# Program order for the first slots, and a weight conversion in two steps, in a delta-rule and MoE kernel

## The chip, the cores and the metric

The kernel runs on one core of one Trainium2 chip. The metric is the device time of one execution in microseconds, the median of three runs. Before the change it is 869.11 us (the three runs: 869.25, 866.1, 869.11). The profile is of another execution, which took 863.97 us and spans 862.2 us from its first to its last instruction.

## What is computed

Two blocks follow each other. The first is a delta-rule recurrence over 768 positions for 4 batches of 8 heads of width 48; the second is a two-layer block with a quick GELU over the 3072 resulting tokens, 384 to 2048 to 384.

```python
for t in range(S):                       # 768 positions, per batch and head
    kt, vt, bt = k_n[:, :, t], v[:, :, t], beta[:, :, t, None]
    y[:, :, t] = einsum('bhd,bhde->bhe', q[:, :, t], state)
    v_old = einsum('bhde,bhd->bhe', state, kt)
    state = state + bt[:, :, :, None] * einsum('bhd,bhe->bhde', kt, vt - v_old)
x = y.transpose(0, 2, 1, 3).reshape(3072, 384)
h = x @ w_in
out = (h / (1 + exp(-1.702 * h))) @ w_out
```

Here k_n is k divided by its norm. The activations q, k, v and beta are float32. The weights w_in and w_out arrive as 64-bit floats[...], so the kernel turns their two 32-bit words into float32 itself.

## The kernel before, in words

The positions are cut into 6 chunks of 128. A **unit** is one chunk of one batch with its 8 heads; there are 24, in the order chunk by chunk, so units 0 to 3 are the first chunk of the four batches, units 4 to 7 the second. Within a chunk the recurrence is solved in 4 blocks of 32 positions.

What a unit needs:

- `normalize` divides its keys by their norms. The first seven units are done on DVE by `normalize_first`; later ones mostly on POOL.
- `prepare` transposes keys and queries on PE (psT), copies them with ACT to kqT, multiplies them (psG) and copies the products to G with ACT or DVE. A part of G goes through DRAM to NT, and POOL masks the rest with affine_select.
- `invert` turns NT into the inverses of the 32 x 32 diagonal blocks, on DVE; they go through DRAM and come back as XB.
- The class `Step` solves the unit: `above` (PE, psR), `rest` (DVE subtracts psR from V), `solve` (PE, psU from XB and V) and `solved` (ACT copies psU to U), block after block; then `state` (PE psS, DVE adds it to S_bd) and `outputs` (PE psY, ACT and DVE copy it to xT, and six small DMAs move some of its rows).
- `hidden` (PE ph from xT and w_in, ACT's GELU to gT) and `written` (PE po from gT and w_out) are the second block. They wait in a list, `queue`, and `take` draws from it by cost.

The loop at the end of the program calls `slot(n)` for n from -1 to 24. A slot has six groups. In it three units are in work side by side: A = unit n-1 (blocks 2 and 3, state, outputs), B_ = unit n (block 1) and D_ = unit n+1 (block 0). Each group also prepares a piece of unit n+4, inverts a piece, converts some weight parts and draws from `queue`; while `queue` is still empty, it issues six bf16 products on the identity (`warm`) that keep PE busy.

**Weights.** w_in is 12 parts of 128 x 512, w_out 16 parts of 128 x 384. `fetch` brings a part's 64-bit words into a stage, most of which lies in the memory of w_out itself, whose final values come later; `taken` records which words of it are in use, and `ahead` fetches a part only if its stage is free. `convert` calls `from_double`, and `made` frees a stage, for most parts one part later. `from_double` is, for a part that is not among the first three: DVE masks the exponent (L167), ACT shifts it and clamps it at zero with a ReLU (L172), DVE builds the mantissa from the high word (L173) and the low word (L174), puts the sign to the exponent (L175) and multiplies the two (L176). The first three parts (`alone`) do the ReLU's work with two DVE operations. `weights(n)` converts n parts and fetches ahead. How many parts are converted where is set by W0 (before the slots), W1 (just before the loop) and WB (slots -1 to 3).

**What sets the order on an engine.** The program's order is not the order of the queues. A scheduler takes the instructions by priority and by when it expects them to be ready, so it moves an instruction ahead of earlier ones that it thinks have to wait. An operation wrapped in `pinned` is kept behind the pinned ones before it on its engine. Before the change only the work of the first chunk's inversion, of `normalize_first`, of the first three conversions and some DMAs are pinned:

```python
def pinned(op):
    return lambda *a, **kw: tc.keep_in_program_order(op(*a, **kw))
```

Pinned instructions carry the wrapper's line, L104, in the profile. As built before, PE's queue holds, after the 48 warm products of `invert`, another 36 of slots -1 and 0, then all of `prepare` for units 4, 5 and 6 with more warm products, and only then the first `solve`. ACT's queue has the same units' copies ahead of the first U.

Of the kernel before, what the change touches and what calls it, by code (L numbers as in the profile page):

```python
# [18 lines left out]
def kernel(  # L19
# [19 lines left out]
    nc = tc.nc  # L39
# [18 lines left out]
    W0, W1, WB = 3, 2, (1, 3, 4, 7, 8)  # L58
# [46 lines left out]

    for i in range(B):
        for t, src, dma in ((KN, k, nc.sync.dma_start), (QP, q, nc.scalar.dma_start)):
            if i < len(t):
                nc.vector.memset(t[i][:, :, D:DP], 0.0)
                load(i, ((t, src),), dma)  # L110
# [21 lines left out]
    def warm(n, after=None):  # L132

        ps = ps_moe.tile([128, 256], F32, tag="moe", name="ps_warm")
        if after is not None:
            after(ps[:, 0:1], 0.0)
        for _ in range(n):
            nc.tensor.matmul(ps, lhsT=ones[:, 0:128], rhs=ones, start=True, stop=True)  # L138
# [11 lines left out]
    def from_double(dst, raw, n, alone):  # L150

        lo, hi = raw[:, :, 0], raw[:, :, 1]
        tmp = wk.tile([128, 2, n], I32, tag="P", name="tmp")
        t0, p = tmp[:, 0], tmp[:, 1]  # L160
        ts, stt = nc.vector.tensor_scalar, nc.vector.scalar_tensor_tensor
        if alone:
            ts, stt = pinned(ts), pinned(stt)
        AND, OR = ALU.bitwise_and, ALU.bitwise_or
        E1 = 1 << 20

        ts(p, hi, 0x7FF * E1, None, op0=AND)  # L167
        if alone:
            ts(p, p, -896.0 * E1, 0.0, op0=ALU.add, op1=ALU.max)
            ts(p, p, 255.0 * E1, 8.0, op0=ALU.min, op1=ALU.mult)  # L170
        else:
            nc.scalar.activation(p, p, ACT.Relu, scale=8.0, bias=low)  # L172
        ts(t0, hi, E1 - 1, E1, op0=AND, op1=OR)  # L173
        stt(out=dst, in0=lo.bitcast(U32), scalar=2.0**-32, in1=t0, op0=ALU.mult, op1=ALU.add)  # L174
        stt(out=p, in0=hi, scalar=-(1 << 31), in1=p, op0=AND, op1=OR)  # L175
        stt(out=dst, in0=dst, scalar=2.0**-20, in1=p.bitcast(F32), op0=ALU.mult, op1=ALU.mult)  # L176
# [16 lines left out]
    stages, taken, made = {}, {}, []  # L193
# [61 lines left out]

    def convert(part):
        if part in stages:
            dst = target(part)
            from_double(dst, stages.pop(part), dst.shape[-1], part < NA)

            made.append(part)
            while made and (len(made) > 1 or part < NA or part >= n_parts - 8):
                taken.pop(made.pop(0), None)
# [5 lines left out]
    def normalize(n):  # L269
# [6 lines left out]
        nc.vector.tensor_reduce(ssq, ksq, axis=AX.X, op=ALU.add)  # L276
# [3 lines left out]
        nc.vector.tensor_scalar(rn, rn, 1e-6, None, op0=ALU.add)  # L280
        nc.vector.reciprocal(rn, rn)
# [3 lines left out]
    def normalize_first(b0, nb=HB):  # L285

        tt, ts = pinned(nc.vector.tensor_tensor), pinned(nc.vector.tensor_scalar)
        red, recip = pinned(nc.vector.tensor_reduce), pinned(nc.vector.reciprocal)
        stt = pinned(nc.vector.scalar_tensor_tensor)
# [21 lines left out]
    def prepare(n):  # L311
# [4 lines left out]
        for i, src in enumerate((kn, qp)):  # L316
# [5 lines left out]
            for j in range(NP):  # L322
                nc.tensor.transpose(psT[:, j, :], flat[:, j * 128 : (j + 1) * 128], ident)  # L323
            nc.scalar.activation(kqT[:, :, i, :], psT, ACT.Copy)  # L324
# [4 lines left out]
        for g in range(0, NP, 2):  # L329
# [4 lines left out]
            for i in range(2):  # L334
                for hh in range(2):
                    pr = slice(hh * 64, hh * 64 + D)
                    nc.tensor.matmul(  # L337
                        ps[hh][:, i], lhsT=kqT[pr, g + i, 0, :], rhs=kqT[pr, g + i, :, :],
                        start=True, stop=True,
                    )  # L340
            nc.scalar.activation(G[:, 2 * g : 2 * g + 4 : 2], ps[0], ACT.Copy)  # L341
            if n < HB or B <= n < 2 * B + HB:
                nc.scalar.activation(G[:, 2 * g + 1 : 2 * g + 4 : 2], ps[1], ACT.Copy)
            else:
                nc.vector.tensor_copy(G[:, 2 * g + 1 : 2 * g + 4 : 2], ps[1])  # L345
# [22 lines left out]
    def invert(c, b0=0, nb=B):  # L368
# [5 lines left out]
        tt, red = nc.vector.tensor_tensor, nc.vector.tensor_reduce  # L374
# [35 lines left out]
        nc.scalar.activation(X1, halves(Y)[1].rearrange("p l i -> p i l"), ACT.Copy)  # L410
# [21 lines left out]
        if c == 0:  # L432
            warm(NY, pinned(nc.vector.memset))
        YS = wk.tile([128, BS, BS], F32, tag="P", name="YS")[part]
        nc.vector.tensor_tensor(YS, Y, bc, op=ALU.mult)
# [21 lines left out]
    class Step:  # L457
# [10 lines left out]
        def with_state(self, ps, i):  # L468
            for j in range(NP):
                nc.tensor.matmul(  # L470
# [8 lines left out]
        def above(self, blk, h):  # L479
            r, a = slice(blk * BS, (blk + 1) * BS), slice(0, blk * BS)  # L480
            nc.tensor.matmul(  # L481
# [4 lines left out]
        def rest(self, blk):  # L486
            r = slice(blk * BS, (blk + 1) * BS)
            if self.c > 0 or blk > 0:
                nc.vector.tensor_tensor(self.V[r], self.V[r], self.psR[r], op=ALU.subtract)  # L489

        def solve(self, blk, h, psU):
            r = slice(blk * BS, (blk + 1) * BS)
            nc.tensor.matmul(  # L493
# [4 lines left out]
        def solved(self, blk, psU):  # L498
            r = slice(blk * BS, (blk + 1) * BS)
            nc.scalar.copy(self.U[r], psU[r])  # L500

        def turned(self, lhsT, rhs, start):

            for h in range(H):
                j, p = h // 2, h % 2 * 64
                nc.tensor.matmul(  # L506
# [13 lines left out]
        def state(self):  # L520
# [3 lines left out]
            for j in range(NP):  # L524
                nc.tensor.matmul(  # L525
# [4 lines left out]
            for hh in range(2):  # L530
                pr = slice(hh * 64, hh * 64 + 64)
                St = S_bd[pr, self.b, :, hh, :]
                nc.vector.tensor_tensor(St, psS[pr, :, hh, :], St, op=ALU.add)

        def outputs(self):
# [6 lines left out]
            other = nc.scalar.copy if self.c == 0 else nc.vector.tensor_copy  # L542
            for hh, copy in ((0, nc.scalar.copy), (1, other)):
# [14 lines left out]
    def hidden(xT, gT, t, cost):  # L558

        n = t.stop - t.start  # L560
        for f0 in range(0, FC, 2):
# [3 lines left out]
            for u in range(2):  # L565
                f = f0 + u
                for j in range(KC):
                    nc.tensor.matmul(  # L568
# [4 lines left out]
            nc.scalar.activation(  # L573
# [3 lines left out]
    def written(c, b0, gT):  # L577

        for i in range(HB):
            b = b0 + i  # L580
            po = ps_moe.tile([128, DM], F32, tag="moe", name="po")
            for f in range(FC):
                nc.tensor.matmul(  # L583
# [6 lines left out]
            nc.vector.tensor_copy(o, po)  # L590
# [166 lines left out]
    for n in range(-1, len(units) + 1):  # L757

# [32 lines left out]
```

## Time and profile before

| engine | busy us | share of the span |
|---|---|---|
| PE, products | 806.3 | 94% |
| PE, weight loads | 597.2 | 69% |
| DVE | 490.7 | 57% |
| ACT | 208.7 | 24% |
| POOL | 105.5 | 12% |

Shares of the whole span hide that the kernel has stages. In the table of busy times by stretch PE is at 0.00 us busy from 40 to 60 us, where DVE inverts the first chunk's blocks, and at 20.00 of 20.00 us in each stretch from 200 to 320 us. By line, the chain of work that ended last is PE ph 29.5%, PE po 28.0%, and for the rest mostly the recurrence's products; DMA of w_out's words has 1.6%. Of the waits, the longest single one on DVE that a conversion causes is 8.1 us, for ACT's ReLU (L172); ACT in turn waited 43.4 us in 14 waits for DVE's mask (L167), which costs nothing where ACT had nothing else to do.

In the profile a row of a timeline gives the start, the duration, the engine and line, what is written from what, how many instructions are merged, and in brackets how long the engine had stood idle before and what released it. PE stands for TensorE's products, PEld for its weight loads.

### The profile page before, as it was taken

How to read it: one execution, taken by the hardware profiler on the slowest of the kernel's cores; microseconds unless marked ns; L12 is line 12 of the kernel's file. 1: busy time of each engine (PE TensorE's matmuls, PEld its weight loads, DVE VectorE, ACT ScalarE, POOL GpSimd, SP SyncE). 2: the span in 40 equal slices, each digit the busy share in tenths (PEclk: the TensorE clock that was granted, in tenths of full speed). 3: DMA queues.
4: the chain of work that ended last, by engine and by line, in shares of the span. 5: the costliest groups of instructions: out<-in, count | busy, mean ns of one | idle time of the engine just before them, and what ended most of it. 6: DMA issues, size and time to landing. Idle time of an engine off the chain costs nothing.

```text
span 862.2 us, 15547 instructions
## 1 busy us (share of the span) xinstructions
PE 806.3 (94%) x6564; PEld 597.2 (69%) x6564; DVE 490.7 (57%) x1024; ACT 208.7 (24%) x407; POOL 105.5 (12%) x117
## 2 busy tenths in 40 slices
PE   8209799989999999999999999999999999999998
PEld 7107678757767867867767767767768768677684
DVE  5897579979982692682782772772862851110100
ACT  3202345433212312312312212212212112112020
POOL 2103131330012102102102101101100000000000
PEclk9759769999999999999999999999999999999999
DMA  9996462541423123132132132042032020000000
GB/s 144 185 165 148 109 162 68 141 112 33 83 60 68 40 58 73 35 73 60 34 76 65 26 85 62 19 85 53 10 78 50 2 57 2 10 14 1 19 5 18
DMA packets 160964, 55.75 MB, mean 65 GB/s; under 512 B 128672, under 2 KB 157568, under 8 KB 160896
## 3 DMA queue, kind: packets, MB, share of 16 engines
q1 hardware_dynamic: 154048, 46.02, 26.1%
q0 software_dynamic: 1856, 7.87, 3.0%
q10 hardware_dynamic: 4992, 0.89, 1.0%
q8 instruction: 51, 0.84, 0.4%
q14 instruction: 17, 0.14, 0.1%
HBM read 33.13 MB, written 20.45 MB: 62 GB/s over the span
## 4 chain that ended last, share of the span: by engine, by line
PE 83%; DVE 8%; DMA 5%; issue 1%; ACT 1%; ACTq 0%; POOL 0%; SPq 0%; DVEq 0%; POOLq 0%
PE ph L568 30%; PE po L583 28%; PE psR L481 5%; PE psY L506 5%; PE psG L337 5%; PE psU L493 4%; PE psR L470 2%; PE psS L525 2%; PE psT L323 2%; DMA w_out<-in_moe_w_out_dram 2%; DMA w_out<-in_moe_w_in_dram 1%; DVE P L104 1%; DMA bI<-in_beta_dram 1%; DVE YB L104 1%; DMA Nd<-G 1%
## 5 line engine op out<-in xcount | busy, mean ns | idle before, releaser
L583 PE MATMUL po<-w_out,gT 128*128 128x384 f32 x768 | 267.4, 494 | 2.1 <-DVE w_out L176 2.1
L568 PE MATMUL ph<-xT,w_in 128*128 128x256 f32 (+1 forms) x1248 | 269.1, 369 | 0.0
L568 PEld LDWEIGHTS ph<-xT,w_in 128*128 128x128 f32 x1248 | 219.1, 191 | 37.1 <-issue 9.5
L583 PEld LDWEIGHTS po<-w_out,gT 128*128 128x128 f32 x768 | 139.9, 190 | 92.3 <-issue 8.5
L573 ACT ACTIVATE gT<-ph 128x512 f32<-128x512 f32 (+1 forms) x104 | 58.6, 564 | 187.7 <-PE ph L568 187.7
L489 DVE TENSOR_TENSOR V<-V,psR 32x384 f32<-32x384 f32 x92 | 50.6, 550 | 92.9 <-PE psR L481 87.1
L500 ACT COPY U<-psU 32x384 f32<-32x384 f32 x96 | 45.0, 469 | 149.2 <-PE psU L493 99.4
L481 PEld LDWEIGHTS psR<-U,G 32*32 32x32 f32 (+2 forms) x1152 | 55.2, 110 | 23.9 <-issue 20.9
L138 PE MATMUL ps_warm<-ident 128*128 128x256 bf16 x260 | 33.9, 289 | 36.1 <-DVE ps_warm L104 33.0
L481 PE MATMUL psR<-U,G 32*32 32x48 f32 (+2 forms) x1152 | 65.7, 209 | 2.0 <-ACT U L500 2.0
L337 PE MATMUL psG<-kqT 48*128 48x256 f32 x384 | 58.4, 406 | 5.1 <-ACT kqT L324 4.0
L493 PEld LDWEIGHTS psU<-V,XB 32*32 32x32 f32 x1536 | 39.8, 110 | 27.7 <-issue 12.5
L361 POOL TENSOR_SCALAR_AFFINE_SELECT G<-G 128x1024 f32<-128x1024 f32 x24 | 26.7, 1111 | 249.8 <-DVE G L345 115.2
L138 PEld LDWEIGHTS <-ident 128*128 128x128 bf16 x260 | 26.3, 104 | 42.4 <-DVE ps_warm L104 34.0
L401 DVE TENSOR_TENSOR P<-NT,YB 64x2 f32<-64x2 f32 (+4 forms) x150 | 51.9, 346 | 4.6
L590 DVE COPY o<-po 128x384 f32<-128x384 f32 x24 | 13.3, 555 | 71.8 <-PE po L583 71.7
L493 PE MATMUL psU<-V,XB 32*32 32x48 f32 x1536 | 48.0, 210 | 3.4 <-DVE V L489 3.4
L405 DVE TENSOR_REDUCE YB<-P 64x2 f32<-64x2 f32 (+4 forms) x150 | 48.0, 320 | 4.5
L341 ACT ACTIVATE G<-psG 128x512 f32<-128x512 f32 x48 | 28.7, 597 | 76.6 <-PE psG L337 76.4
L337 PEld LDWEIGHTS psG<-kqT 48*128 48x128 f32 x384 | 35.4, 188 | 14.3 <-ACT kqT L324 5.4
L545 DVE COPY last<-psY 48x128 f32<-48x128 f32 x20 | 5.9, 294 | 59.1 <-ACT xT L546 58.2
L377 DVE TENSOR_TENSOR NT<-NT,bI 64x1024 f32<-64x1024 f32 x10 | 12.2, 1220 | 43.8 <-DMA NT<-Nd 43.7
(81 smaller groups left out, 715.3 us busy)
## 6 DMA issues: line engine op xcount, KB each, us to landing
Nd<-G SPq DMA_DIRECT2D x24, 512.0 KB, 3.2
w_out<-in_moe_w_out_dram POOLq DMA_DIRECT2D x14, 384.0 KB, 4.1
KN<-in_k_dram SPq DMA_DIRECT2D x24, 192.0 KB, 3.1
V<-in_v_dram SPq DMA_DIRECT2D x24, 192.0 KB, 3.1
out_dram<-o SPq DMA_DIRECT2D x24, 192.0 KB, 1.9
QP<-in_q_dram SPq DMA_DIRECT2D x20, 192.0 KB, 3.1
w_out<-in_moe_w_in_dram SPq DMA_DIRECT2D x6, 576.0 KB, 11.7
NT<-Nd SPq DMA_DIRECT2D x24, 128.0 KB, 2.5
```

Source lines behind the costliest of these rows:

```text
L138: nc.tensor.matmul(ps, lhsT=ones[:, 0:128], rhs=ones, start=True, stop=True)
L337: nc.tensor.matmul(ps[hh][:, i], lhsT=kqT[pr, g + i, 0, :], rhs=kqT[pr, g + i, :, :], start=True, stop=True,)
L401: tt(P, diag(Nf, i * BS, [[0, i], [1, i]]), diag(Yf, 0, [[BS, i], [1, i]]), op=ALU.mult,)
L405: red(diag(Yf, i, [[BS, i]]), P, axis=AX.X, op=ALU.add, negate=True)
L481: nc.tensor.matmul(self.psR[r, h, :], lhsT=self.G[a, h, 0, r], rhs=self.U[a, h, :], start=(self.c == 0 and h == 0), stop=True, skip_group_ ...
L489: nc.vector.tensor_tensor(self.V[r], self.V[r], self.psR[r], op=ALU.subtract)
L493: nc.tensor.matmul(psU[r, h, :], lhsT=self.XB[r, h, :], rhs=self.V[r, h, :], start=True, stop=True,)
L500: nc.scalar.copy(self.U[r], psU[r])
L506: nc.tensor.matmul(self.psY[p : p + D, j, :], lhsT=lhsT(h), rhs=rhs(h), start=start and j == 0, stop=True, skip_group_check=True,)
L568: nc.tensor.matmul(ph[:, u], lhsT=w_in[:, j, f * 128 : (f + 1) * 128], rhs=xT[:, j, t], start=(j == 0), stop=(j == KC - 1),)
L573: nc.scalar.activation(gT[f0 // FQ][:, f0 % FQ : f0 % FQ + 2, t], ph, ACT.Gelu_apprx_sigmoid)
L583: nc.tensor.matmul(po, lhsT=gT[f // FQ][:, f % FQ, i * C : (i + 1) * C], rhs=w_out[:, f, :], start=(f == 0), stop=(f == FC - 1),)
```

## The change

First, the slots of n = -1, 0 and 1 are issued in the program's order on PE, DVE and ACT: a small class wraps the three engines and pins each operation while a flag is set. POOL and the DMA queues keep their scheduled order.

Second, `from_double` becomes a generator of two steps. The first is the mask and the ReLU, which now write into the part's final place (`dst`) instead of a temporary; the second is the rest, with a temporary of half the size. `convert(part)` takes the first step of the next part that is staged before it takes the second step of its own. A first step of a w_out part is put off if its place is still a stage in use.

Third, the counts W1 and WB are changed: one part less just before the loop, one part more in slot 1. The aim is that the recurrence of the first units doesn't stand behind work that the scheduler put ahead of it, and that DVE doesn't stand waiting for the ReLU of the part it is converting.

```diff
-    W0, W1, WB = 3, 2, (1, 3, 4, 7, 8)
+    W0, W1, WB = 3, 1, (1, 3, 5, 7, 8)
...
+    in_order = [False]
+    class Engine:
+        def __init__(self, engine):
+            self.engine = engine
+        def __getattr__(self, name):
+            op = getattr(self.engine, name)
+            return pinned(op) if in_order[0] else op
+    vec, act, pe = Engine(nc.vector), Engine(nc.scalar), Engine(nc.tensor)
...
-        tmp = wk.tile([128, 2, n], I32, tag="P", name="tmp")
-        t0, p = tmp[:, 0], tmp[:, 1]
+        p = dst.bitcast(I32)
         ts(p, hi, 0x7FF * E1, None, op0=AND)
...
-            nc.scalar.activation(p, p, ACT.Relu, scale=8.0, bias=low)
-        ts(t0, hi, E1 - 1, E1, op0=AND, op1=OR)
-        stt(out=dst, in0=lo.bitcast(U32), scalar=2.0**-32, in1=t0, op0=ALU.mult, op1=ALU.add)
+            act.activation(p, p, ACT.Relu, scale=8.0, bias=low)
+        yield
+        t = wk.tile([128, n], I32, tag="P", name="tmp")
+        f = t.bitcast(F32)
+        ts(t, hi, E1 - 1, E1, op0=AND, op1=OR)
+        stt(out=f, in0=lo.bitcast(U32), scalar=2.0**-32, in1=t, op0=ALU.mult, op1=ALU.add)
         stt(out=p, in0=hi, scalar=-(1 << 31), in1=p, op0=AND, op1=OR)
-        stt(out=dst, in0=dst, scalar=2.0**-20, in1=p.bitcast(F32), op0=ALU.mult, op1=ALU.mult)
+        stt(out=dst, in0=f, scalar=2.0**-20, in1=dst, op0=ALU.mult, op1=ALU.mult)
+        yield
...
+    def begin(part):
+        if part not in begun:
+            if part >= parts_in:
+                a, b = (part - parts_in) * DM, (part - parts_in + 1) * DM
+                if any(taken[p][0] < b and a < taken[p][1] for p in stages if p in taken):
+                    return
+            dst = target(part)
+            begun[part] = from_double(dst, stages[part], dst.shape[-1], part < NA)
+            next(begun[part])
     def convert(part):
         if part in stages:
-            dst = target(part)
-            from_double(dst, stages.pop(part), dst.shape[-1], part < NA)
+            begin(part)
+            if staged:
+                begin(min(staged))
+            stages.pop(part)
+            next(begun.pop(part))
...
     for n in range(-1, len(units) + 1):
+        in_order[0] = n < HB
         slot(n, 15.6 if n <= B else 18.8 if n <= B + HB else 20.8)
```

In the rest of the diff `nc.vector`, `nc.scalar` and `nc.tensor` become `vec`, `act` and `pe`, from `normalize` to `written`.

As built, the new queues read so. PE, after the 48 warm products: 18 of slot -1's, the first solve, 18 more, unit 4's transposes, 6 warm, psR, and so on, each slot's preparation lying between links of the chain. DVE: two whole conversions and a mask, V, three conversions, V twice, one conversion, V, two conversions, S_bd. ACT: a ReLU or a copy in the order of the program, so the first U stands behind two ReLUs, and the first xT copies behind a ReLU of w_out. From slot 2 on the scheduler orders again; it puts masks of w_out parts ahead of V subtractions there.

## The prediction

> **What bounds the kernel now.** I read the page's 40 slices first, to see where TensorE (PE) is not full. One slice is 862.2 / 40 = 21.6 us.
>
> ```profile
> PE   8209799989999999999999999999999999999998
> DVE  5897579979982692682782772772862851110100
> PEclk9759769999999999999999999999999999999999
> ```
>
> From the tenth slice on PE is full at full clock; what is left there is PE work, and a change can only move when that stretch begins. The losses lie in the first nine slices, 0 to 195 us. The table of busy times by stretch takes them apart (columns: stretch, length, then busy time and count of PE, PE loads, DVE, ACT, POOL, granted clock, DMA share, GB/s):
>
> ```profile
> 64.00:95.80 31.80, 27.96 (x219) 22.14 (x219) 22.62 (x50) 10.74 (x19) 8.60 (x14) 0.95 0.64 139
> 95.80:116.00 20.20, 14.90 (x218) 12.86 (x216) 13.50 (x27) 7.37 (x16) 4.30 (x8) 0.58 0.44 134
> 112.00:181.90 69.90, 67.72 (x673) 54.01 (x673) 61.45 (x137) 32.10 (x68) 18.71 (x21) 0.93 0.48 122
> 181.90:201.70 19.80, 17.71 (x155) 10.78 (x155) 15.67 (x43) 6.21 (x14) 5.29 (x5) 1.00 0.41 98
> ```
>
> Between 95.8 and 116 PE is 74% busy at a clock of 0.58; this is the recurrence of units 0 and 1, a chain of small products, V subtractions on VectorE (DVE) and U copies on ScalarE (ACT). From 112 to 182 DVE is 88% busy, and near the end PE waits for converted w_out. The timelines of SyncE, PE and DVE show when the chain could start and did:
>
> ```profile
> 69.39 2.60 SPq L104 DMA_DIRECT2D XB<-Yd  x4
> ...
> 64.01 10.68 PE L138 MATMUL ps_warm<-ident 128*128 128x256 bf16 x83 [32.97 <-DVE ps_warm L104]
> ...
> 95.91 0.86 PE L493 MATMUL psU<-V,XB 32*32 32x48 f32 x16
> 110.55 2.02 PE L525 MATMUL psS<-U,KN 128*128 128x96 f32 x8 [0.75 <-ACT U L500]
> ...
> 90.81 1.07 DVE L175 SCALAR_TENSOR_TENSOR tmp<-w_out,tmp 128x512 int32<-128x512 int32 x1 [8.10 <-ACT tmp L172]
> 112.68 0.72 DVE L533 TENSOR_TENSOR S_bd<-psS,S_bd 64x192 f32<-64x192 f32 x2 [1.30 <-PE psS L525]
> ```
>
> XB's four transfers take 3.0 us each at the median, so the first has landed at 69.39 + 3.0 = 72.4. The first solve, psU, runs only at 95.91: the scheduler put units 4, 5 and 6's transposes, psG products and all of slot -1 and 0's warm products ahead of it. Meanwhile DVE stood 8.10 us for a ReLU on ACT that sat behind prepare's copies. So a ready chain lies 23.5 us in a queue, DVE loses 8.1 us, and the clock falls because the warm products are used up before the chain. I then followed the chain of waits from 146 us; it runs through DVE and w_out fetches:
>
> ```profile
> 168.50 4.56 DMA w_out<-in_moe_w_out_dram
> 175.64 4.98 DMA w_out<-in_moe_w_out_dram
> 184.00 4.04 DMA w_out<-in_moe_w_out_dram
> 190.77 0.91 PE po L583 x2
> ```
>
> After 190.77 it stays on PE to the end.
>
> **What the Trainium skill says.** "TensorE: Matmul & The Clock Gate", section "Architectural detail": ACT and DVE are strict FIFOs, PE may only pull weight loads forward. So order is all: a head that waits holds everything behind it. The 8.10 us row and the late psU agree. The same page, section "What's actually happening": PE's clock is halved after an idle window of some 3.4 us and restored by sustained work. The trace agrees on the two levels (warm products from 64 us: 0.50 for two us, 0.75, then 1.00; 0.50 from 98 to 113 us with PE about 75% busy), and shows that small gaps suffice. "Perfetto Trace Analysis", section "Optimization Strategy": where regimes differ, interleave them. That is what the new order does with prepare, warm and chain.
>
> **The change, part by part.** *The split conversion.* Five DVE operations and a ReLU stay; no instruction goes or comes. From DVE rows, a w_in part is 0.42 + 0.42 + 3 x 0.69 = 2.9 us (75.46 to 78.36 in the trace), a w_out part 2 x 0.35 + 3 x 0.55 = 2.35. The first step (mask, ReLU) now runs one part earlier and writes p into the target instead of tmp, so about 2.5 us of DVE work lie between mask and its reader. The ReLU is 0.72 us. This removes the 8.10 us wait. A begin can now wait for a fetch at the head of DVE; see below.
>
> *W1 and WB.* 2+1+3+4+7+8 = 1+1+3+5+7+8 = 25 parts: no total changes, one conversion moves from before the slots to slot 1.
>
> *Slots in program order.* Nothing is removed; warm products (24 in 2.73 us, 0.114 each) move between chain links. I walk the new queues with the old durations.
> - PE: 48 + 18 warm from 64.0, at 10.68 / 83 each, 8.5 us: 72.5. XB is there at 72.4: solve at 72.5, 23.4 us earlier. U's copy on ACT stands behind two ReLUs, done by 74.4, so U is at 74.9. Then 18 warm 2.1, unit 4's transposes 1.0, 6 warm 0.7, psR 0.9: 78.0.
> - DVE: the keys' normalization ends at 73.2; two parts lie ahead of the first V: 73.2 + 5.8 = 79.0. V 0.6, three parts 8.7: 88.3. Behind this V wait the next psU and, through U, psR on PE; PE has psG (1.1 + 1.6), warms and 18 more warm, so its psR is done at 86.9 and it is DVE that sets 88.3.
> - V 0.6; PE's 32 interleaved products and a wait 1.4; V 0.6; one part 2.9; V 0.6; two parts 5.8; S_bd 0.7: 100.9 us.
> - PE over the same stretch: 72.5 plus about 26.5 us of products and warms, 99: nearly full, so I take full clock. ACT has about 15 us in it; its ReLU heads wait only for masks already past.
>
> S_bd of unit 0 ends at 113.4 before, so 12.5 us are won there. First ph: before at 121.77. After: S_bd 100.9, a mask 0.35 and w_out's ReLU 0.6 ahead of the xT copies (1.4): 103.3; six small DMAs took 3.8 us to issue and 1.8 to land: 108 to 109. About 13 us, less 24 products of psU (1.1 us), which now follow. Units 4 to 6 are prepared by then in both.
>
> *Debts.* At S_bd the old DVE had four of five operations of the ninth part behind it, the new one only begins it: 0.42 + 3 x 0.69 - 0.69 = 1.8 us. Up to YS of units 4 and 5 (156.9 us before) the new order also holds three masks and three sign operations more (3 x 0.9 = 2.7), work done ahead that comes back later. A begin of a w_out part stands before a V of slot 2; its fetch follows unit 5's affine_select and the ninth and tenth part's last read (99.5), and with 4.1 us to landing comes at 104.6, where DVE is at 103.7: 0.9, or 2 if the fetch takes 5.2 (the raw rows). DVE shift: 12.5 - 1.8 - 0.9 to 2 = 9 to 10, of which up to 2.7 is borrowed for a while.
>
> *The stretch to 190.* If DVE and fetches are 9 to 10 us earlier, so is each link, since the fetches wait for conversions. I cost this at nothing else: the parts' spacing and buffers are as before. PE is 11 to 12 ahead and may lose the rest waiting for w_out. I take 9: 869.1 - 9 = 860.1.
>
> **The rivals.**
> 1. *Main: shift of 9 carried to the end*, 860. For it: DVE 88% busy and on the chain from 146 on; PE full after 192.
> 2. *The w_out fetches hold the end of the stretch.* Three transfers of 4 to 5 us and a 3.65 us issue gap stand in 25 us of the chain; POOL's order has changed, and a begin waiting for a fetch blocks DVE. Some 5.5 of 9 us are lost: 865.5. Against: the fetches are released by conversions that come earlier.
> 3. *PE carries its whole lead.* Besides 11 to 12 us, it wins back half clock (119 to 125 us at 0.50: 3 us) and 2.8 us of waits at 181, 183 and 190: up to 14: 855. Against: DVE supplies w_out.
> 4. *Program order hurts: slower.* Four V subtractions and four U copies are pinned behind conversions and ReLUs. If each of the four V waits costs a part more than walked, 4 x 2.9 = 11.6 us, S_bd comes at 112.5, and the debts of 1.8 + 2.7 are left, with half clock: 869.1 + 4 = 873. Against: the walk has each wait already, and 23 us of head start.
>
> **How the numbers follow.** Chances: 0.62 for 860, 0.14 for 865.5, 0.13 for 855, 0.11 for 873. The three runs before lie within 866.1 to 869.25, so a median carries 2 us of noise. The range, 854 to 867, holds main, most of 2 and most of 3, and leaves out the slower case. 0.5% is 4.3 us, a bound at 864.8: faster has main, 3 and 0.05 of 2, 0.80; same takes the rest of 2 and a little, 0.10; slower 0.10.
>
> **What would show it.** First psU near 72.5; the first V near 79; S_bd near 101; first ph near 108; clock 1.00 from 75 to 125 us; no 8 us wait of DVE for a ReLU; the last PE wait for w_out near 181 instead of 190. It is wrong if V subtractions wait behind conversions for more than walked, if DVE stands several us before a w_out mask, or if the first 195 us are won and PE shows new idle time after 200.

## The result, and the profile after

The changed kernel takes **857.33 us** (median of 4 runs, 854.72 to 859.25) beside 867.88 us for the kernel before (median of 4, 866.1 to 869.25): a ratio of **0.9878**, 95% interval 0.9842 to 0.9913, some 10.5 us less. 860 was predicted, in a range of 854 to 867. The profiled run took 854.72 us and spans 853.0 us, 9.2 less than the span before, so a difference of two traces has 9.2 us to account for. By the page, PE's products are busy for 803.8 us instead of 806.3 and PE is idle for 853.0 - 803.8 = 49.2 us instead of 862.2 - 806.3 = 55.9: 6.7 us less idle time, and 2.5 us less busy time for the same 6564 products.

The page's 40 slices of the changed kernel (a slice is 853.0 / 40 = 21.3 us):

```profile
PE   8309989999999999999999999999999999999998
DVE  5899899879882872862872862862862840110100
PEclk9759899999999999999999999999999999999999
```

Slices 5 and 6, from 85 to 128 us, have 8 and 9 tenths of the clock where they had 7 and 6, and PE is at 9 from the seventh slice on. The table of busy times by stretch of the changed kernel (columns as before: stretch, length, PE, PE loads, DVE, ACT, POOL, clock, DMA share, GB/s):

```profile
95.80:116.00 20.20, 17.62 (x207) 13.88 (x204) 18.36 (x43) 11.82 (x23) 6.04 (x9) 0.84 0.73 216
112.00:181.90 69.90, 67.77 (x650) 52.34 (x650) 60.24 (x128) 27.64 (x60) 19.69 (x20) 0.98 0.48 112
181.90:201.70 19.80, 18.50 (x126) 13.11 (x126) 18.47 (x49) 6.32 (x14) 3.41 (x3) 1.00 0.16 40
```

In the first row DVE is busy for 18.36 us instead of 13.50, since conversions now lie between the links of the chain of units 0 and 1, where before it mostly waited for psR, and the clock is 0.84 instead of 0.58. The DMA engines carry 216 GB/s instead of 134. The timelines of PE and DVE, with the answers to the lines shown of before:

```profile
73.61 0.83 PE L104 MATMUL psU<-V,XB 32*32 32x48 f32 x16 [0.20 <-DMA XB<-Yd]
...
90.21 0.23 PE L104 MATMUL psU<-V,XB 32*32 32x48 f32 x1 [1.90 <-DVE V L104]
...
92.08 1.44 PE L104 MATMUL ps_warm<-ident 128*128 128x256 bf16 x6
...
111.88 5.38 PE L599 MATMUL ph<-xT,w_in 128*128 128x128 f32 x30 [2.15 <-DMA xT<-last]
...
183.97 0.91 PE L614 MATMUL po<-w_out,gT 128*128 128x384 f32 x2 [1.30 <-DVE w_out L192]
...
82.98 1.74 DVE L104 SCALAR_TENSOR_TENSOR tmp<-w_out,tmp 128x512 f32<-128x512 uint32 x1
...
85.43 0.69 DVE L104 SCALAR_TENSOR_TENSOR w_in<-w_out,w_in 128x512 int32<-128x512 int32 x1 [0.71 <-ACT w_in L104]
...
89.60 0.55 DVE L104 TENSOR_TENSOR V<-V,psR 32x384 f32<-32x384 f32 x1
...
102.03 0.72 DVE L104 TENSOR_TENSOR S_bd<-psS,S_bd 64x192 f32<-64x192 f32 x2
```

The first solve comes at 73.61 us instead of 95.91, released by XB's landing and not by a queue. DVE's wait of 8.10 us for a ReLU has become one of 0.71. Unit 0's state is done at 102.03 + 0.72 = 102.75 instead of 113.40, the first ph starts at 111.88 instead of 121.77, and the last wait for w_out ends at 183.97 instead of 190.77. The lead is thus 22.3 us at the solve, 10.7 at the state, 9.9 at ph and 6.8 at the last w_out wait. It shrinks so much from solve to state because the chain itself became slower: that distance is 29.1 us instead of 17.5, with conversions and preparation now lying between its links. After the last wait for w_out PE has no wait in either kernel. The first group of 18 ph products in that stretch starts at 193.87 instead of 201.70 in the chain that ended last (7.8 us earlier); from about 290 us on the lead is 9.2 us, and so it stays to the end. The chain of waits of the changed kernel still runs through fetches:

```profile
107.52 4.32 DMA xT<-last
...
161.04 4.81 DMA w_out<-in_moe_w_out_dram
...
176.54 4.37 DMA w_out<-in_moe_w_out_dram
```

New in it is the transfer of xT, 4.32 us from issue to landing, right ahead of the first ph.

### The profile page after: what moved, and what is told of

The parts are those of the page before. It is cut to its first block, busy times and chain, and to the rows that moved or that the text cites. A ratio compares the mean times of both kernels' runs of the same rounds, so it can differ in the third digit from the quotient of the medians.

```text
span 853.0 us, 15548 instructions
## 1 busy us (share of the span) xinstructions
PE 803.8 (94%) x6564; PEld 593.6 (70%) x6564; DVE 495.7 (58%) x1024; ACT 208.5 (24%) x407; POOL 107.2 (13%) x117
## 4 chain that ended last, share of the span: by engine, by line
PE 83%; DVE 8%; DMA 6%; issue 1%; POOL 0%; ACT 0%; ACTq 0%; SPq 0%; DVEq 0%; POOLq 0%
PE ph L599 29%; PE po L614 28%; PE psY L537 5%; PE psR L512 4%; PE psG L368 4%; PE psU L524 4%; PE psR L501 2%; DVE P L104 2%; PE psT L354 2%; PE psS L556 2%; DMA w_out<-in_moe_w_out_dram 2%; DVE YB L104 1%; DMA w_out<-in_moe_w_in_dram 1%; PE ps_warm L104 1%; DMA bI<-in_beta_dram 1%
## 5 line engine op out<-in xcount | busy, mean ns | idle before, releaser
L512 PEld LDWEIGHTS psR<-U,G 64*32 64x32 f32 (+2 forms) x1088 | 49.9, 107 | 20.9 <-issue 19.4
L512 PE MATMUL psR<-U,G 64*32 64x48 f32 (+2 forms) x1088 | 59.7, 205 | 0.4 <-ACT U L531 0.4
L152 PE MATMUL ps_warm<-ident 128*128 128x256 bf16 x152 | 22.5, 315 | 35.1 <-DVE ps_warm L104 32.8
L368 PE MATMUL psG<-kqT 48*128 48x256 f32 x352 | 53.9, 407 | 0.3 <-DVE G L376 0.3
L524 PEld LDWEIGHTS psU<-V,XB 32*32 32x32 f32 x1424 | 34.3, 105 | 22.1 <-issue 9.8
L432 DVE TENSOR_TENSOR P<-NT,YB 64x2 f32<-64x2 f32 (+4 forms) x135 | 46.2, 342 | 4.3
L436 DVE TENSOR_REDUCE YB<-P 64x2 f32<-64x2 f32 (+4 forms) x135 | 43.3, 321 | 4.3
L152 PEld LDWEIGHTS <-ident 128*128 128x128 bf16 x152 | 16.9, 113 | 39.5 <-DVE ps_warm L104 33.2
L524 PE MATMUL psU<-V,XB 32*32 32x48 f32 x1424 | 41.3, 203 | 1.2 <-DVE V L520 1.2
L304 POOL TENSOR_TENSOR ksq<-KN 128x384 f32<-128x384 f32 x17 | 14.8, 868 | 175.9 <-DMA KN<-in_k_dram 175.9
```

Of the source, the lines that this page charges most:

```text
L152: pe.matmul(ps, lhsT=ones[:, 0:128], rhs=ones, start=True, stop=True)
L368: pe.matmul(ps[hh][:, i], lhsT=kqT[pr, g + i, 0, :], rhs=kqT[pr, g + i, :, :], start=True, stop=True,)
L432: tt(P, diag(Nf, i * BS, [[0, i], [1, i]]), diag(Yf, 0, [[BS, i], [1, i]]), op=ALU.mult,)
L436: red(diag(Yf, i, [[BS, i]]), P, axis=AX.X, op=ALU.add, negate=True)
L512: pe.matmul(self.psR[r, h, :], lhsT=self.G[a, h, 0, r], rhs=self.U[a, h, :], start=(self.c == 0 and h == 0), stop=True, skip_group_check=True,
L524: pe.matmul(psU[r, h, :], lhsT=self.XB[r, h, :], rhs=self.V[r, h, :], start=True, stop=True,)
```

## The experiments

Theory A is the prediction's: the gain is an earlier chain of units 0 and 1, for which the order of the program must hold on all three queues and the conversion must be split, so that DVE doesn't pay for the order with waits for its own ReLUs; from about 112 us on PE is nearly full and carries what was won. Rival B says that the rate at which weights are fetched and converted sets the stretch up to 190 us, and that fetches, counts or DVE's work decide what is left of the lead.

Ratios are to the kernel before, timed on the same chip. The last three columns are from each run's trace: first solve, end of unit 0's state, first ph. The traces start the chain up to 2.8 us apart for reasons upstream of the change, so the distance between the columns says more than the columns. Each trace is one execution: the four of the changed kernel spread from 854.72 to 859.25 us, and the traced one is the fastest.

| kernel | ratio (95%) | solve | state | ph |
|---|---|---|---|---|
| before | 1 | 95.91 | 113.40 | 121.77 |
| changed | 0.9878 (0.9842-0.9913) | 73.61 | 102.75 | 111.88 |
| e1 split alone | 1.0027 (1.0010-1.0044) | 96.18 | 114.25 | 122.12 |
| e2 order alone | 0.9958 (0.9941-0.9975) | 75.53 | 110.40 | 118.85 |
| e3 counts alone | 0.9998 (0.9982-1.0014) | 97.75 | 115.18 | 123.53 |
| e4 order on PE only, with split | 1.0115 (1.0093-1.0137) | 75.27 | 120.03 | 127.67 |
| e12 order to slot 0, with split | 1.0025 (1.0009-1.0040) | 74.67 | 110.14 | 120.09 |
| e9 order to slot 3, with split | 1.0229 (1.0187-1.0272) | 76.18 | 105.43 | 117.93 |
| e5 no warm products | 0.9921 (0.9908-0.9934) | 75.21 | 106.92 | 115.81 |
| e6 counts 1,2,6,7,8 | 0.9893 (0.9874-0.9913) | 74.02 | 101.61 | 110.04 |
| e7 counts 1,2,4,9,8 | 0.9969 (0.9954-0.9983) | 76.18 | 101.99 | 110.83 |
| e8 fetches in order | 0.9929 (0.9911-0.9948) | 76.40 | 105.19 | 112.85 |
| e10 select twice | 0.9948 (0.9931-0.9964) | 74.83 | 107.34 | 115.09 |
| e11 conversion cut | 0.9963 (0.9947-0.9978) | 75.45 | 105.74 | 115.42 |

### One part alone

**e1: the split and the new counts, without the program's order.**

```diff
-        in_order[0] = n < HB
+        in_order[0] = False
```

> The new conversion and the new counts, but no slot pinned: PE's queue again holds units 4, 5 and 6's preparation ahead of the first solve. My theory (the order of PE's queue starts the chain): first psU stays near 95, S_bd of unit 0 near 110 to 113, and the gain is at most the 2 to 3 us that DVE wins by no longer standing 8.1 us for the ReLU: 865 to 868. Rival (the removed ReLU wait is what counts, since DVE is busy from there to 190 us): DVE's 8.1 us come through whole: 858 to 860.

869.88 us. The timelines of PE and DVE of e1:

```profile
96.18 0.86 PE L524 MATMUL psU<-V,XB 32*32 32x48 f32 x16
...
92.07 1.67 DVE L191 SCALAR_TENSOR_TENSOR w_in<-w_out,w_in 128x512 int32<-128x512 int32 x2 [4.75 <-ACT w_in L185]
```

The solve stays where it was, and the split doesn't even take the wait away: 4.75 and another 1.07 us are left of 8.10, because ACT's queue still has six copies of later units (86.15 to 91.4 us) ahead of the next three ReLUs. One part's distance on DVE is no help if ACT is behind by more than a part.

**e2: the order and the new counts, without the split.** Mask and ReLU of a part stand directly before the rest of it.

```diff
             begin(part)
-            if staged:
-                begin(min(staged))
             stages.pop(part)
```

> The slots pinned and the new counts, but a part's mask and ReLU stand directly before the rest of its conversion again. My theory: first psU near 73.5 as in the changed kernel; each conversion in the pinned slots now waits for its own ReLU, 0.7 us or more where a copy is ahead of it on ACT, 9 parts by 0.4 to 1.5 us: S_bd near 107 to 112, total 860 to 864. Rival (the split is what counts): the DVE queue in program order stalls by 8 us or more, and the time is 867 to 873.

865.17 us. The longest of DVE's waits in the timeline of e2:

```profile
87.35 0.69 DVE L104 SCALAR_TENSOR_TENSOR w_in<-w_out,w_in 128x512 int32<-128x512 int32 x1 [4.48 <-ACT w_in L104]
```

The solve is at 75.53, but from there to the end of the state it takes 34.9 us, where the changed kernel needs 29.1. DVE's waits for ReLUs in between are 0.46 + 4.48 + 1.64 + 1.30 = 7.9 us, against 0.71. That is 7.2 us more of waits, enough for these 5.8; e1 shows that the split has no such worth without the order.

**e3: the new counts in the kernel before.**

```diff
-    W0, W1, WB = 3, 2, (1, 3, 4, 7, 8)
+    W0, W1, WB = 3, 1, (1, 3, 5, 7, 8)
```

> Only the counts W1 and WB of the kernel before are changed. My theory: the same 25 parts, so no change: 866 to 869. Rival (one conversion less before the slots frees DVE and ACT for the first unit): 863 to 865.

866.88 us, no change; the ReLU wait is 8.11 us, and solve and ph are both 1.8 us later, at the same distance. Split and counts +0.3%, order and counts -0.4%, counts 0.0%, all three -1.2%: the gain belongs to the combination of order and split. Whether these two need the new counts was not run; e6 and e7 vary the counts under them.

**e4: the order on PE's queue alone.**

```diff
-    vec, act, pe = Engine(nc.vector), Engine(nc.scalar), Engine(nc.tensor)
+    vec, act, pe = nc.vector, nc.scalar, Engine(nc.tensor)
```

> As the changed kernel, but only PE's queue keeps the program's order in slots -1 to 1; DVE and ACT are ordered by the scheduler. My theory (PE's order is the lever, and the rest follows what PE delivers): 856 to 860. Rival (without their order DVE and ACT let V and U stand behind conversions and copies): S_bd later than 106 and 861 to 866.

876.77 us, 1.15% slower than before. PE and DVE in the timeline of e4:

```profile
93.11 1.48 PE L104 MATMUL psR<-U,G 32*32 32x48 f32 x16 [13.38 <-ACT U L531]
...
99.91 0.55 DVE L520 TENSOR_TENSOR V<-V,psR 32x384 f32<-32x384 f32 x1
```

PE solves at 75.27 and then stands 13.38 us for the U copy, which ACT does at 92.61 behind seven ReLUs (77.08 to 92.7 us) that in turn wait for masks on DVE; the first V is at 99.91 instead of 78.88. PE is busy for 12.65 of the 28.5 us from 72.5 to 101, DVE for 26.47, with conversions. A strict order on one queue of a chain that crosses three makes that queue wait for the other two.

### How many slots

**e12: the order for slots -1 and 0 only.**

```diff
-        in_order[0] = n < HB
+        in_order[0] = n < HB - 1
```

> Program order for slots -1 and 0 alone; slot 1, in which unit 0's blocks 2 and 3, its state and its xT copies lie, is left to the scheduler. Split conversion and counts as in the changed kernel. Theory (the gain comes from the whole chain of units 0 and 1 up to the xT copies standing ahead of conversions and of later units' preparation): psU of unit 0 still at 73 to 77 us, but in slot 1 V subtractions and xT copies stand behind work put ahead of them again; S_bd at 104 to 110, ph at 115 to 120, ratio to before 0.992 to 1.0, that is 861 to 868 us. Rival (the early start of the first solve and the split are what counts, slot 1's order is worth nothing): S_bd at 100 to 103, ph at 110 to 113, ratio 0.985 to 0.991, or below if the scheduler fills slot 1 better.

868.87 us. DVE and PE in the timeline of e12:

```profile
81.60 0.43 DVE L180 TENSOR_SCALAR w_in<-w_out 128x512 int32<-128x512 int32 x1 [2.64 <-DMA w_out<-in_moe_w_in_dram]
...
85.82 1.49 PE L104 MATMUL psR<-U,G 32*32 32x48 f32 x16 [6.71 <-ACT U L104]
```

The mask at 81.60 carries its own line (L180) and not L104: it is work of slot 1, no longer in order, which the scheduler put among the pinned instructions of slot 0. It waits 2.64 us for its words; its ReLU, and that of the next part, whose mask waits too (0.72 us), sit ahead of the first U copy on ACT, and PE waits 6.71 us for that copy. Pinning orders only the pinned; loose work may still be put in front of it. Slot 1 is needed, and the numbers of the theory that says so (state 104 to 110, ph 115 to 120) are met within 0.2 us; the time, 868.87, lies just above its 861 to 868.

**e9: the order for slots 2 and 3 as well** (HB is 2; the expectation calls them slots 2 to 5).

```diff
-        in_order[0] = n < HB
+        in_order[0] = n < 2 * HB
```

> The program order is kept for slots 2 to 5 as well (n < 2*HB instead of n < HB). Theory A (from about 112 us PE is nearly full, so order has little left to win there, but fixed heads can block): masks of w_out then stand on DVE in the program's place, behind them V; each fetch that lands late (0.7 to 1.6 us in three places in the changed kernel) holds V and all behind it. Ratio to before 0.985 to 0.995, that is 855 to 863 us, ph still at 111 to 114 us. Rival (the scheduler's order in slots 2 and 3 still costs several us, as it did in slots 0 and 1): 846 to 852 us, ratio below 0.981, with fewer PE waits between 112 and 184 us than the changed kernel's 3.4 us.

887.11 us, worse than both theories said, and the worst kernel here. ACT and PE in the timeline of e9:

```profile
155.58 0.62 ACT L104 ACTIVATE w_out<-w_out,low 128x384 int32<-128x384 int32 x1 [9.06 <-DVE w_out L104]
...
162.85 4.49 PE L104 MATMUL ph<-xT,w_in 128*128 128x128 f32 x24 [10.28 <-DMA xT<-last]
```

In slot 2's program order DVE updates S_bd and inverts blocks of units 4 and 5 (7.5 us without a gap from 147.7 to 155.2) before it masks the next w_out part; ACT's ReLU waits 9.06 us at the head of its queue with the copies of xT behind it, and PE waits 10.28 us for xT. Between 112 and 184 us PE is busy for 51.46 of 72 us, against 68.57 in the changed kernel. The program's order is better than the scheduler's in slots -1 to 1 taken together, and much worse in slots 2 and 3. Which of these two slots costs more was not run.

### Counts, fetches and warm products

**e5: no warm products in the slots from -1 to 1.**

```diff
-        if not queue and n <= HB:
+        if not queue and n == HB:
```

> As the changed kernel, without the warm products of slots -1, 0 and 1 (15 groups of 6; the result does not use them). Theory A (DVE sets the pace of the chain, and the warm products are needed to hold PE's clock): the clock falls to 0.50 from about 78 us, the chain's products take twice as long, S_bd at 103 to 106, time 858 to 862. Rival B (the 10 us of warm products in PE's queue delay the chain, which the clock doesn't repay): S_bd near 98 to 100, time 853 to 856.

859.37 us, 0.44% over the changed kernel's ratio, about 4 us, though the two intervals still touch. It leaves out 18 groups of six (PE's count falls from 6564 to 6456), not 15. The stretch from 72.5 to 101 us, first of the changed kernel, then of e5 (columns as before):

```profile
72.50:101.00 28.50, 26.40 (x319) 20.25 (x317) 25.25 (x45) 14.23 (x28) 11.02 (x17) 0.88 0.59 140
72.50:101.00 28.50, 20.91 (x191) 15.80 (x188) 22.55 (x48) 11.69 (x21) 9.04 (x15) 0.59 0.52 108
```

The clock is 0.59 instead of 0.88, psG takes longer (up to 2.56 us for a group of eight instead of 1.13 to 2.08), and the state comes 31.7 us after the solve instead of 29.1. So the warm products seem worth their place, but the larger part of the gain is there without them.

**e6: one conversion less in slot 0, one more in slot 1.**

```diff
-    W0, W1, WB = 3, 1, (1, 3, 5, 7, 8)
+    W0, W1, WB = 3, 1, (1, 2, 6, 7, 8)
```

> As the changed kernel, with counts (1, 2, 6, 7, 8): one conversion moved from ahead of the second V subtraction to behind it. Theory A (PE's 1.9 us wait for that V at 88.3, which also drops the clock to 0.50 until 98, comes from the three conversions ahead of V): that V ends near 87.5, no half clock at 92 to 98, first ph 1 to 3 us earlier, time 854 to 857. Rival B (DVE's sum to S_bd is the same, so nothing moves): S_bd near 102, 857 to 858.

856.66 us (853.92 to 860.26), ratio 0.9893: not to be told from the changed kernel. The same stretch in e6:

```profile
72.50:101.00 28.50, 27.74 (x368) 21.81 (x365) 25.31 (x47) 16.01 (x29) 12.10 (x19) 1.00 0.68 161
```

Here the clock is 1.00, PE has no wait for the second V, the state comes 27.6 us after the solve and ph at 110.04, 1.8 us ahead of the changed kernel. At the end 0.8 us of that is left by the spans (852.2 instead of 853.0): PE waits 2.80 us at 152.23 for KN, which POOL normalizes for a later unit, and later 0.47, 0.92 and 0.53 for w_out.

**e7: one conversion less in slot 0 and in slot 1, two more in slot 2.**

```diff
-    W0, W1, WB = 3, 1, (1, 3, 5, 7, 8)
+    W0, W1, WB = 3, 1, (1, 2, 4, 9, 8)
```

> As the changed kernel, with counts (1, 2, 4, 9, 8): two conversions moved from ahead of S_bd to slot 2, behind it. Theory A (DVE's sum ahead of S_bd sets the start of ph, and PE sets the end from there): S_bd near 97, ph near 107 to 108, time 852 to 855. Rival B (DVE and the fetches of w_out, which hang on conversions, set the time up to 184 us): S_bd comes earlier but PE's waits for w_out grow by as much, 857 to 859.

864.36 us. The state comes 25.8 us after the solve, the best of all, and ph at 110.83; then the parts that are missing come due. DVE in the timeline of e7:

```profile
189.29 0.36 DVE L180 TENSOR_SCALAR w_out<-w_out 128x384 int32<-128x384 int32 x1 [4.69 <-DMA w_out<-in_moe_w_out_dram]
```

PE's waits for w_out are 2.99 + 0.42 + 1.54 + 3.07 = 8.0 us in place of the changed kernel's 2.2. This is Rival B, and by more than its 857 to 859: with later conversions the last fetch of w_out is issued at 184.30 instead of 176.54, and the supply of w_out holds the end of the stretch.

**e8: the fetches of weights in the program's order on POOL.**

```diff
-    def weights(n, dma=nc.gpsimd.dma_start):
+    def weights(n, dma=pinned(nc.gpsimd.dma_start)):
```

> As the changed kernel, with the weight fetches on POOL's queue in the program's order, so that the two raw parts needed last are fetched last instead of at 102 us. Theory A (the six small xT transfers took 4.3 us to land instead of 1.8 because of the fetches beside them, and PE stood 2.15 us for them): they land by 110, time 855 to 857. Rival B (the xT transfers are late because of their issue behind ACT's ReLU, or the fetches that matter are behind others in POOL's queue): ph near 112 or later, 857 to 862.

860.68 us. PE in the timeline of e8:

```profile
93.02 0.23 PE L104 MATMUL psU<-V,XB 32*32 32x48 f32 x1 [1.90 <-DVE V L104]
...
94.89 0.83 PE L104 MATMUL ps_warm<-ident 128*128 128x256 bf16 x6
```

The distance from solve to state is 28.8 us, like the changed kernel's. PE's queue is the same as there up to 105 us, with the same wait of 1.90 us for the second V; but here the clock stays at 1.00 behind it, and the six warm products take 0.83 us instead of 1.44. From that psU to the state it is 12.2 us instead of 12.5, so the changed kernel's stretch of half clock cost its chain some 0.4 us. Later, fetches bunch: the DMA engines are busy for 0.95 of the time from 101 to 116 us (0.75 in the changed kernel), DVE waits 3.71 us for w_out's words at 184.12, and PE 2.99 us at 155.78 for POOL's KN. By the medians the end moves by some 4 us, at the edge of the two intervals. Rival B's numbers are met (ph 112.85, 857 to 862 us), and the scheduled order is not the worse one.

### Two costs by themselves

**e10: each affine_select of `prepare` twice.**

```diff
         nc.gpsimd.affine_select(out=G[:, :, 1, :], in_=G[:, :, 1, :], ...)
+        nc.gpsimd.affine_select(out=G[:, :, 1, :], in_=G[:, :, 1, :], ...)
```

> Each of the 24 affine_selects on POOL is issued twice; the second changes no value. It measures by itself what DVE pays for a POOL instruction beside it. In the changed kernel's trace, DVE instructions that meet an affine_select took 1.2 to 1.7 us instead of 0.4 to 0.7. Theory of contention: with 24 more POOL instructions of 1.13 us, DVE's busy time (436 us from 72.5 us on) grows by some 10 to 24 us at the same count of instructions. Rival (the long rows are something else, such as DMA writes): DVE's busy time stays within 3 us. The time itself: PE hides most of it, 857 to 862 us; where contention strikes the chain before 112 us, ph comes 1 to 3 us later.

862.08 us. As built, the queues of PE, DVE and ACT hold the same instructions in the same order as the changed kernel's; only POOL's differs. DVE's busy time goes from 495.7 to 504.7 us, 9.0 more with the same 1024 instructions (9.1 more from 72.5 us on), a little under the expected 10 to 24. The time is at the upper edge of the expected 857 to 862. The costliest groups by shape, first of the changed kernel, then of e10 (count, then busy us and mean ns of one, then idle before and its causes):

```profile
L415 DVE TENSOR_TENSOR P<-NT 64x768 f32<-64x768 f32 x9 | 8.5, 948 | 0.0
L416 DVE TENSOR_REDUCE NT<-P 64x64 f32<-64x768 f32 x9 | 8.5, 940 | 0.0
L520 DVE TENSOR_TENSOR V<-V,psR 32x384 f32<-32x384 f32 x88 | 48.4, 550 | 89.9 <-PE psR L512 84.0 <-PE psR L501 4.5
L104 DVE TENSOR_SCALAR w_in<-w_in 128x512 int32<-128x512 int32 x6 | 3.3, 556 | 0.2
```

```profile
L419 DVE TENSOR_TENSOR P<-NT 64x768 f32<-64x768 f32 x9 | 13.9, 1542 | 0.0
L420 DVE TENSOR_REDUCE NT<-P 64x64 f32<-64x768 f32 x9 | 8.5, 940 | 0.0
L104 DVE TENSOR_SCALAR w_in<-w_in 128x512 int32<-128x512 int32 x6 | 4.9, 810 | 0.2
L524 DVE TENSOR_TENSOR V<-V,psR 32x384 f32<-32x384 f32 x88 | 48.4, 550 | 88.5 <-PE psR L516 82.5 <-PE psR L505 4.5
```

The products of two tensors in SBUF and the one-tensor operations on SBUF of the conversion pay; reductions (940 ns in both kernels) and the subtractions that read psR from PSUM (550 ns in both) don't. In e10 13 reductions and 4 operations that read PSUM ran beside a select, and none was longer. For the products this agrees with the Trainium skill, "SBUF — State Buffer", section "Who interferes with whom": a VectorE instruction with two SBUF inputs contends with a GpSimd instruction that reads SBUF, and one of the two waits for the other to end. The masks have one input, so that statement doesn't cover them. It isn't always DVE that pays: at 84.20 us in e10 a DVE operation keeps its 0.69 us, and the select that starts at 84.27 takes 1.58 us where most take 1.09. Of 9.0 us more, 5.1 are in the one shape P<-NT 64x768 (8.5 to 13.9 in the group shown, less 0.3 in a single instruction of L104), which in the later slots falls onto the second select (POOL at 310.30, 373.20 and 437.40 us). In the stretch of units 0 and 1 the price falls on the chain: solve to state is 32.5 us instead of 29.1.

**e11: for w_out, the last operation of a conversion is left out.**

```diff
-        stt(out=dst, in0=f, scalar=2.0**-20, in1=dst, op0=ALU.mult, op1=ALU.mult)
+        if dst.shape[-1] != DM:
+            stt(out=dst, in0=f, scalar=2.0**-20, in1=dst, op0=ALU.mult, op1=ALU.mult)
```

> For w_out's 16 parts the last DVE operation (mantissa times exponent, L192) is left out, so w_out holds only sign and exponent and the result is not the reference's. DVE loses 16 x 0.55 to 0.67 = 9 to 10.5 us between 100 and 190 us, and no engine gets more work. Theory A (from 112 us on PE is nearly full, 68.6 of 72 us): at most the 2.2 us of w_out waits and a us of V waits are won, 853.5 to 857 us. Rival (DVE's conversion rate still sets the stretch to 184 us): 847 to 852 us, ratio to before 0.976 to 0.982.

864.14 us: slower than the changed kernel by about 0.9% with less work, which neither theory allows. DVE is busy for 486.8 us instead of 495.7, as computed. But the program handed to the scheduler is another one: up to 114 us DVE's queue is the changed kernel's, and PE's and ACT's even longer, and from there on its choices differ. ACT and PE in the timeline of e11:

```profile
134.52 0.66 ACT L442 ACTIVATE NT<-YB 64x256 f32<-64x256 f32 x1 [2.29 <-DVE YB L104]
...
138.01 1.13 PE L369 MATMUL psG<-kqT 48*128 48x256 f32 x8 [1.95 <-ACT kqT L356]
```

Here ACT's copy of YB and a w_out ReLU stand ahead of unit 1's xT copies (135.59 to 136.85) and of a later unit's kqT; in the changed kernel both come after the first half of the xT copies, which start at 129.49. PE then waits 1.95, 0.42 and 0.79 us between 136 and 144 us, is busy for 4.84 of these 8 us, and its clock is 0.77 and 0.80 in that stretch and the next (1.00 in the changed kernel). Of the 10.0 us by which this trace is longer, 3.5 are there at the first ph, with the queues still the same (the chain began 1.8 us later), and the rest comes after it. The order in slot 2 is the likely cause of that rest; no run isolates it. So e11 doesn't tell whether DVE's rate sets the stretch. None of the twelve kernels is measurably faster than the changed one.

## Why the prediction was right, point by point

- **The head start is set by XB: right.** psU at 72.5 was predicted, 73.61 measured; the first V at 79.0, measured 78.88.
- **"Three parts 8.7: 88.3": too small by 1.3.** The second V came at 89.60. DVE set it, as said, but two terms were missing, of which a part that took 2.73 us instead of 2.9 gave a little back: an operation of 0.69 us took 1.74 beside POOL's affine_select (83.06 to 84.17), and the mask-to-reader distance left a ReLU wait of 0.71, since U copies and unit 4's copies were ahead of that ReLU on ACT. e10 shows that such meetings with POOL cost DVE time.
- **"S_bd 100.9": measured 102.75.** Besides the 1.3, V waited 0.42 us for psR where no wait was walked (the 1.00 us ahead of the V before it was in the walk, at 1.4), and a mask of 0.42 us took 1.32 beside the second affine_select (98.13 to 99.34).
- **"Nearly full, so I take full clock": wrong for about 7 us, and again for 3.4 behind ph.** PE's products did fit. But PE stood 1.90 us ahead of 90.21, and the six warm products at 92.08 took 1.44 us instead of 0.82: half clock until about 99. The table by stretch has it (from 92 us on, in the changed kernel):

```profile
92.00:94.00 2.00, 2.00 (x15) 1.28 (x14) 1.93 (x5) 1.69 (x3) 0.00 (x0) 0.53 0.01 4
94.00:96.00 2.00, 2.00 (x18) 1.71 (x18) 1.55 (x4) 0.00 (x0) 1.11 (x2) 0.50 0.29 58
96.00:98.00 2.00, 2.00 (x12) 0.96 (x8) 1.93 (x4) 1.03 (x3) 0.00 (x0) 0.50 0.82 335
```

In e6, without that wait, the clock is 1.00 and the state 1.5 us closer to the solve. But e8 has the wait and keeps 1.00, and wins only some 0.4 us by it. So the prediction's "small gaps suffice" holds for some executions and not for others, and most of what e6 wins must come from the missing wait itself or from what lies around it.
- **"First ph 108 to 109": measured 111.88.** The copies of xT ended at 104.96, not 103.3, as ACT waited 1.55 us for the mask ahead of them. The six issues took 5.40 us instead of 3.8. The first product started 2.5 us after the last issue; one of the transfers took 4.32 us where 1.8 was assumed. The DMA engines were busy for 0.89 of that stretch (103.5 to 111.9), at 271 GB/s, while before the change it was 0.73 and 227 GB/s (114.8 to 121.8). The earlier chain met the w_out fetches that the same conversions release. That the transfers share the DMA engines is the likely cause; e8, with a share of 0.95, still had a wait of 1.65 us for xT, and no run changed the load by itself.
- **"0.9, or 2" of DVE standing for a w_out mask at 104: did not happen.** The masks at 102.78 and 106.25 found their words. In e5, e6 and e8 the wait is there, with 1.40, 0.88 and 0.70 us.
- **"No 8 us wait for a ReLU": right,** and e1 and e2 show that it takes both parts: each alone leaves a wait of over 4 us (4.75 and 4.48), both together 0.71.
- **"Last PE wait for w_out near 181": measured 183.97.** The lead at the YS of units 4 and 5 was 4.5 us (its end at 152.36 instead of 156.88), where 9 to 10 less 2.7 was forecast. Of the 2 to 3 us that are missing there, 1.9 were missing at S_bd already. From S_bd to that YS DVE does 98 instructions instead of 85 and is busy for 45.2 us instead of 39.0: nine operations of conversions more (3.9 us), which the forecast had at 1.8 + 2.7, and four others, two V subtractions among them, which it had not. At 184 us, where the lead is 6.8, part of this work done ahead seems to have come back.
- **"Shift of 9 carried to the end": the number is right, with 9.2 by the spans,** 10.5 by the medians, and luck has a part in it. The lead of PE at ph was 9.9 us instead of about 13, and less of it was lost on the way than the forecast allowed: two errors that cancel. Nor was the 9 carried unbroken: the lead is 6.8 us at the last w_out wait and 7.8 ten us later. The step from there to 9.2 is not a wait and is over by about 290 us: from 193.87 (201.70 before) to the end PE is busy for 655.7 us instead of 657.0, without a gap. What made the products cheaper isn't settled. The order in which the scheduler mixes them there is another one, and no run tests that.
- **The rivals.** Fetches (2) do take hold as soon as conversions slip: e7, 864.36 us, lies close to the 865.5 of that rival. PE carrying its whole lead (3) was not seen. The slower case (4) is what happens if the order is on one queue (e4: 876.77), or in too many slots (e9: 887.11): V and U did wait for more than walked, by 13.4 us for a single U.

## What to carry to other kernels

Where a scheduler puts ready work behind other work, fix the order of the whole chain on every engine that it crosses, and only for the stretch where you have seen the scheduler lose: one queue alone (+1.15%), one slot too few (+0.25%) and two slots too many (+2.3%) all left this kernel slower than it was before the change. A fixed order turns each producer's delay into a wait of everything behind it, so put distance between an operation and its reader on another engine at the same time. When a chain moves earlier, look again at what it now runs beside: another engine's work on the same memory, and the transfers that its own work sets off.

## What the runs showed of the hardware that was not expected

- A DVE operation on SBUF that met a POOL affine_select often ended later by about the length of the meeting: 0.69 us became 1.74 and 0.42 became 1.32 beside selects of 1.11 and 1.21 us. Not all did: at 119.05 us in the changed kernel one kept its 0.54 us, and the select beside it took 1.47. 24 more selects cost DVE 9.0 us in e10, with its queue unchanged; the reductions and the operations reading PSUM that met one (13 and 4) were not longer.
- The same wait of PE can be followed by half clock or not. 1.90 us, ended at 90.21, was followed in the changed kernel by 0.53, 0.50, 0.50 and 0.76 in the stretches of two us from 92 to 100; in e8, with the same queue on PE and the same 1.90 us, ended at 93.02, the clock stayed at 1.00. The 2.15 us ahead of ph at 111.88 were followed by 0.65 and 0.50 from 112 to 116, with PE full; 2.80 us in e6, ended at 152.23, were not followed by half clock. What decides isn't shown here.
- Executions of one program differ in this clock: the four of the changed kernel have a mean of 0.972, 0.968, 0.969 and 0.964 and take 854.72, 856.64, 858.01 and 859.25 us. A difference of a few us between two single traces may be no more than this.
- Leaving out 16 operations on DVE went with a slower kernel (e11, by about 0.9%), in which the rest was put in another order.
